# First layer, chunks 1 to 7: the next chunk's decoding asked for behind the first gate step instead of in front of it

## The chip, the cores and the metric

The kernel runs on one core of a Trainium2 chip. A core has five engines that work side by side, each through a queue of its own in the order in which its instructions stand there: PE (TensorE, matrix products), DVE (VectorE), ACT (ScalarE), POOL (GpSimd) and SP, which here only starts transfers. They meet through semaphores. The metric is the device time of one execution in microseconds (us); a smaller number is better.

## What is computed

Three things stand behind one another: attention over 4 batches of 8 heads (576 positions of 64 each) with a bias worked out from cumulative sums, then a gated feed-forward layer, then a second feed-forward layer. All of it is in single precision.

```
x = attention(q, k, v, s)                  # (4, 8, 576, 64)
x = x.transpose(0, 2, 1, 3)                # 2304 tokens x 512
g = x @ w_gate                             # first layer, 512 -> 1536
x = silu(g) * (x @ w_val) @ w_out          # 1536 -> 512
h = x @ w_in                               # second layer, 512 -> 2048
out = silu(h) @ w_out2                     # 2048 -> 512
```

## The kernel before, in words

PE reaches single precision with split operands: a number is held as a high and a low part, and a product takes three matmuls (lines 522, 523 and 524 in mm3). Weights are split into such parts in the kernel, and they arrive in a packed 64-bit form that must be decoded first.

The first layer goes batch by batch. Each batch has nine chunks of weights (L1): gv 0 to 2, o1 0, gv 3 and 4, o1 1, gv 5, o1 2. A gv chunk is four gate steps of 24 matmuls: twelve into a gate tile, twelve into a value tile (both named pgv, lines 522 to 524), 288 tokens wide. Behind a step come the activation (silu_mul: tanh on ACT, L532, then two products on DVE, L533 on the gate tile and L534 on the value tile) and the split of the result (ACT L112, POOL L536). An o1 chunk is eight down steps of 12 matmuls into tiles po, added up by ACT (L563) or DVE (L565). Chunks 0 to 8 belong to the first batch; in it the weights of each chunk are decoded and split, and stored to memory for the later batches, which only load them.

The attention of the next batch is worked on beside the first layer. At the start of a chunk PE computes one set of scores (psc, L218), which DVE scales, biases and reduces (L235, with a small second instruction per pass that reads the accumulator out); the exponentials are ACT's (L255). Score tiles have banks of their own. In chunks 2, 4 and 6 a set is taken in six DVE operations, in chunks 1, 3, 5 and 7 in ten.

The decoding of one chunk is asked for in w_ahead (w_split for the chunk after the running one, w_load for the one behind that). It has four pieces; a piece is two ACT instructions (L409, then L410 into a scratch tile dk) and two DVE instructions (L412 on dk, then L415, which ends the use of dk). Two cuts follow: a high part by ACT (L112, tile wt from wraw) and a low part by POOL (L501), and then two stores. For chunks 1 to 8 the scratch dk lies in PSUM, in a pool of four banks (ps_m) that gives pgv, po and dk their banks in turn, in the order in which the program asks for them:

```
        if 0 < c < len(L1):
            k = ps_m.tile([P, DW], F32, tag="m", name="dk").bitcast(U32)
        else:
            k = dec_p.tile([P, DW], U32, tag="dk", name="dk")
```

A tile may be written once whatever read the tile before it in that bank is done. PE's order is written out by hand in this part; ACT, DVE, POOL and SP are put in order by a scheduler, which takes its ranks from the order in which the program asks. The chunks' steps and the requests between them are listed in body, which the diff touches.

Of the kernel before, what the change touches and what calls it, by code (L numbers as in the profile page):

```python
# [66 lines left out]
def kernel(  # L67
# [305 lines left out]
    L1 = [("gv", 0), ("gv", 1), ("gv", 2), ("o1", 0), ("gv", 3), ("gv", 4), ("o1", 1), ("gv", 5), ("o1", 2)]  # L373
# [200 lines left out]
    def chunk_steps(c):  # L574
        kind, i = stream[c]
        if c == 0:
            return [lambda f=f, n=n: gate(c, f, f, *n) for f, n in ((1, both[0]), (0, both[1]), (1, both[1]))]
        if kind == "gv":
            return [lambda f=f, n=n: gate(c, 2 * i + f, f, *n) for f, n in order(2, both, "01"[i == NGV - 1])]
        return [lambda m=m, n=n: down(c, i, m, *n) for m, n in order(KD, both, "1")]  # L580
# [162 lines left out]
    def scores(u):  # L743
        x = units[u]
        fetch(u)
        if (*x, "e") not in st:
            masks(*x)
        score_mm(*x)
        for i in HALF[x[2]][0]:
            for f in (score_min, expo, inverse, first_keys, normal):  # L750
                f(*x, i)

    def transpose(u):
        turn_mm(*units[u])
        turned(*units[u], 0)
        turned(*units[u], 1)

    def value(u):
        value_mm(*units[u])
        x_high(*units[u])  # L760
        x_low(*units[u])
# [50 lines left out]
    def w_ahead(c):  # L812
        wst.pop(c - 1, None)
        if first[c + 1]:
            w_split(c + 1)
        else:
            w_load(c + 1)
        if first[c + 2]:
            w_load(c + 2)

    def body():
# [60 lines left out]
        for c in range(last):  # L882
            b = batch[c]
            cur = chunk_steps(c)
            at = {k: [] for k in range(5)}
            if b + 1 < B:
                k, u0 = c % len(L1), (b + 1) * H
                if k < H:
                    at[1 if c == 0 else 0].append(lambda x=u0 + k: scores(x))
                    if k > 1:  # L890
                        at[2].append(lambda x=u0 + k - 2: value(x))
                    if k > 0:
                        at[2].append(lambda x=u0 + k - 1: transpose(x))
                else:
                    at[1] += [lambda x=u0 + k - 2: value(x), lambda x=u0 + k - 1: transpose(x)]
                    at[3].append(lambda x=u0 + k - 1: value(x))
            for n, stp in enumerate(cur):
                if n == 0:
                    w_ahead(c)
                if n * 4 % len(cur) == 0:  # L900
                    todo = events.get(c * 4 + n * 4 // len(cur), [])
                    with tc.issue_after(w_last[0]) if todo else nullcontext():
                        with tc.issue_after(act_last[0]) if todo else nullcontext():
                            for f in todo:
                                f()
                if c == 0:
                    for p in at[n - 1] if n else []:
                        p()
                elif n * 4 % len(cur) == 0:
                    for p in at[n * 4 // len(cur)]:  # L910
                        p()
                stp()
            for p in at[4]:
                p()
# [107 lines left out]
        second_layer.close()  # L1022

    body()


# [42 lines left out]
```

## Time and profile before

| | us |
|---|---|
| time, median of 3 runs | 1009.34 |
| lowest and highest of the three | 1008.01, 1009.38 |
| the profiled execution, its own time | 1008.46 |
| span of that execution in the trace | 1006.1 |
| PE busy in the span | 989.1 (98%) |
| DVE, ACT, POOL busy | 560.2, 523.1, 592.1 |

The span starts with the first instruction in the trace and ends with the last; the execution's own time has 2.36 us around it. A time in a row is counted from the span's start. On the page, part 1 gives busy time, part 2 the same in 40 slices, part 4 the chain of work that ended last, and part 5 groups of instructions with the idle time before them and what ended it. The stretch that the change touches is the first batch's first layer, from 76 to about 202 us.

### The profile page before, as it was taken

The numbers are of one execution on the slowest core, as the hardware profiler recorded it, in microseconds if no ns is written. First come the engines' busy times: TensorE is split into PE (matmuls) and PEld (weight loads), VectorE is DVE, ScalarE is ACT, GpSimd is POOL, SyncE is SP. The second block draws the span as 40 slices with busy tenths as digits, with TensorE's granted clock in tenths as the row PEclk, the third lists the DMA queues.
The fourth block names the chain that finished last, engine by engine and source line by source line (L and its number), as shares of the span: only waits on it lengthen the run. The fifth ranks groups of instructions, "written<-read, shape, count | busy, mean of one in ns | idle before, by whom it ended". The sixth has DMA issues, their size and how long they took to land.

```text
span 1006.1 us, 19498 instructions
## 1 busy us (share of the span) xinstructions
PE 989.1 (98%) x6924; PEld 929.8 (92%) x6924; DVE 560.2 (56%) x1408; ACT 523.1 (52%) x1267; POOL 592.1 (59%) x748
## 2 busy tenths in 40 slices
PE   8998999999999999999999999999999999999998
PEld 6587889999898899899899999999999999999998
DVE  5878666635545544545542223366666667665555
ACT  5879887525766435665542543244534335543333
POOL 6966747515866655756551665356567458674445
PEclk9999999999999999999999999999999999999999
DMA  8898879667788799776768686797867866896662
GB/s 232 204 309 293 269 280 303 226 211 252 282 289 268 262 308 303 270 241 229 261 235 312 248 305 253 264 386 290 292 232 279 316 222 250 295 345 232 248 221 103
DMA packets 81617, 267.16 MB, mean 266 GB/s; under 512 B 9904, under 2 KB 29360, under 8 KB 66160
## 3 DMA queue, kind: packets, MB, share of 16 engines
q1 hardware_dynamic: 81376, 265.73, 75.6%
q8 instruction: 54, 0.88, 0.3%
q14 instruction: 43, 0.35, 0.1%
q10 hardware_dynamic: 144, 0.20, 0.1%
HBM read 208.15 MB, written 57.75 MB: 264 GB/s over the span
## 4 chain that ended last, share of the span: by engine, by line
PE 89%; ACT 4%; DVE 2%; issue 2%; DMA 2%; POOL 1%; POOLq 0%; DVEq 0%; ACTq 0%
PE pgv L522 9%; PE pgv L524 9%; PE pgv L523 9%; PE pu L664 6%; PE pu L668 6%; PE pu L667 6%; PE po L709 6%; PE po L710 6%; PE po L711 6%; PE po L522 5%; PE po L523 5%; PE po L524 5%; PE pv L351 4%; PE psc L218 4%; PE ptr L302 3%
## 5 line engine op out<-in xcount | busy, mean ns | idle before, releaser
L522 PE MATMUL pgv<-xt,wt 128*128 128x288 f32 x768 | 229.9, 299 | 4.6 <-DVE u L533 2.3
L524 PE MATMUL pgv<-xt,wt 128*128 128x288 f32 x768 | 226.2, 294 | 0.0
L523 PE MATMUL pgv<-xt,wt 128*128 128x288 f32 x768 | 226.1, 294 | 0.0
L522 PEld LDWEIGHTS pgv<-xt,wt 128*128 128x128 f32 x768 | 144.1, 188 | 16.4 <-DVE m L235 6.3
L641 POOL TENSOR_TENSOR h<-u,h 128x384 fp32r<-128x384 f32 x72 | 75.1, 1044 | 142.8 <-ACT h L112 134.9
L523 PEld LDWEIGHTS pgv<-xt,wt 128*128 128x128 f32 x768 | 144.1, 188 | 0.0
L524 PEld LDWEIGHTS pgv<-xt,wt 128*128 128x128 f32 x768 | 144.0, 188 | 0.0
L536 POOL TENSOR_TENSOR h<-u,h 128x288 fp32r<-128x288 f32 x96 | 79.1, 826 | 86.2 <-ACT h L112 84.6
L112 ACT ACTIVATE h<-u 128x288 fp32r<-128x288 f32 (+1 forms) x168 | 79.7, 475 | 96.3 <-DVE u L534 95.2
L522 PE MATMUL po<-h,wt 128*128 128x288 f32 x384 | 114.8, 299 | 0.0
L523 PE MATMUL po<-h,wt 128*128 128x288 f32 x384 | 113.1, 294 | 0.0
L524 PE MATMUL po<-h,wt 128*128 128x288 f32 x384 | 113.0, 294 | 0.0
L709 PE MATMUL po<-h,wt 128*128 128x384 f32 x336 | 112.4, 335 | 0.0
L664 PE MATMUL pu<-x,wt 128*128 128x384 f32 x330 | 111.8, 339 | 0.5 <-ACT s L670 0.5
L710 PE MATMUL po<-h,wt 128*128 128x384 f32 x336 | 112.3, 334 | 0.0
L711 PE MATMUL po<-h,wt 128*128 128x384 f32 x336 | 112.3, 334 | 0.0
L667 PE MATMUL pu<-x,wt 128*128 128x384 f32 x330 | 111.7, 339 | 0.0
L668 PE MATMUL pu<-x,wt 128*128 128x384 f32 x330 | 111.7, 339 | 0.0
L641 POOL TENSOR_TENSOR h<-t,h 128x384 fp32r<-128x384 f32 x96 | 106.6, 1131 | 5.5 <-ACT h L112 5.5
L255 ACT ACTIVATE e<-e,m 64x64 f32<-64x64 f32 (+4 forms) x160 | 88.3, 553 | 31.0 <-DVE m L235 30.2
L670 ACT ACTIVATE s<-pu 128x384 f32<-128x384 f32 x48 | 23.6, 492 | 150.5 <-PE pu L668 150.5
L720 DVE TENSOR_TENSOR acc<-po,acc 128x384 f32<-128x384 f32 x144 | 76.8, 558 | 36.3 <-PE po L711 35.6
(115 smaller groups left out, 2187.9 us busy)
## 6 DMA issues: line engine op xcount, KB each, us to landing
wt<-w_d SPq DMA_DIRECT2D x54, 1024.0 KB, 7.0
wt<-wu_d SPq DMA_DIRECT2D x48, 1024.0 KB, 9.3
wt<-wu_d SPq DMA_DIRECT2D x47, 768.0 KB, 6.5
r<-in_w_dram SPq DMA_DIRECT2D x36, 512.0 KB, 7.1
w_d<-wt SPq DMA_DIRECT2D x18, 1024.0 KB, 8.3
r<-in_w_dram SPq DMA_DIRECT2D x64, 256.0 KB, 7.3
qkr<-in_qk_dram SPq DMA_DIRECT2D x32, 288.0 KB, 8.2
cumb<-cum_d SPq DMA_DIRECT2D x15, 576.0 KB, 9.1
```

Source lines behind the costliest of these rows:

```text
L112: act_last[:] = [nc.scalar.activation(out=out, in_=in_, func=AF.Copy, scale=scale).ins]
L255: nc.scalar.activation(out=e[:r, hd, :wd], in_=e[:r, hd, :wd], func=AF.Exp, bias=m[hd][:r], scale=-1.0, accum_out=put[hd],)
L522: nc.tensor.matmul(out=ps[:, :n], lhsT=a, rhs=xh, start=(k == 0), stop=False)
L523: nc.tensor.matmul(out=ps[:, :n], lhsT=a, rhs=xl, start=False, stop=False)
L524: nc.tensor.matmul(out=ps[:, :n], lhsT=c, rhs=xh, start=False, stop=(k == last))
L641: nc.gpsimd.tensor_tensor(out=h[:, 1], in0=u, in1=h[:, 0].bitcast(F32), op=ALU.subtract)
L664: nc.tensor.matmul(out=o, lhsT=a, rhs=x[:, 0, kk], start=fresh and kk == 0, stop=False, skip_group_check=True)
L667: nc.tensor.matmul(out=o, lhsT=a, rhs=x[:, 1, kk], stop=False, **more)
L668: nc.tensor.matmul(out=o, lhsT=c, rhs=x[:, 0, kk], stop=kk == 1, **more)
L709: nc.tensor.matmul(out=ps, lhsT=a, rhs=h[:, 0], start=fresh, stop=False, skip_group_check=True)
L710: nc.tensor.matmul(out=ps, lhsT=a, rhs=h[:, 1], stop=False, **more)
L711: nc.tensor.matmul(out=ps, lhsT=c, rhs=h[:, 0], stop=e == 1, **more)
```

## The change

In each of the chunks 1 to 7 the request w_ahead(c) moves from in front of the chunk's first step to behind it. Since the next batch's score set is asked for with the first step, w_ahead(c) now also stands behind that set. Chunk 0 and all chunks from 8 on are as before. Nothing is added or taken away.

```
             for n, stp in enumerate(cur):
-                if n == 0:
+                if n == (1 if 0 < c < len(L1) - 1 else 0):
                     w_ahead(c)
                 if n * 4 % len(cur) == 0:
```

PE's instructions stand in the same order in both kernels. On DVE, ACT, POOL and SP the order differs between chunk 1 and chunk 8 and nowhere else. Since the banks are given out in the order of the requests, they differ too. Before, chunk 1 asks for four dk tiles and then for the two tiles of its first step, so the first step lies in banks that a dk has used, and so does the second. In the changed kernel the first step asks first, then the four dk tiles, then the second step: six requests over four banks, so that the second step gets the two banks of the first step, and what it waits for is L533 and L534 of that step. It is so in chunks 1, 2, 4, 5 and 7.

DVE in chunk 5, the part of its queue that ends with the first step's L533; e and m are the scores' results, wraw the decoded weights, r a packed piece. Before:

```order
L235 ISA m 128x1
L235 ISA e,m<-psc,e 128x64
L235 ISA m 128x1
L235 ISA e,m<-psc,e 128x64
L235 ISA m 128x1
L235 ISA e,m<-psc,cumb,m 128x448
L235 ISA m 128x1
L235 ISA e,m<-psc,e,m 128x64
L235 ISA m 128x1
L235 ISA e,m<-psc,cumb,m 128x448
L235 ISA m 128x1
L533 SCALAR_TENSOR_TENSOR u<-th,pgv 128x288
```

In the changed kernel, the rows that end with the same L533:

```order
L235 ISA m 128x1
L235 ISA e,m<-psc,e 128x64
L235 ISA m 128x1
L415 SCALAR_TENSOR_TENSOR wraw<-r_2198,dk 128x512
L235 ISA e,m<-psc,cumb,m 128x448
L235 ISA m 128x1
L412 SCALAR_TENSOR_TENSOR dk<-wraw,dk 128x512
L235 ISA e,m<-psc,e,m 128x64
L235 ISA m 128x1
L235 ISA e,m<-psc,cumb,m 128x448
L235 ISA m 128x1
L533 SCALAR_TENSOR_TENSOR u<-th,pgv 128x288
```

Before, the four decoded pieces of this chunk's turn stand wholly ahead of the rows shown; the last of their L415 comes right behind the set's first score pass. Now three L412 and two L415 stand among the set's first nine score passes, all ahead of L533, and one L412 and two L415 behind it.

DVE in chunk 2, at the score operations on 320 columns and the first step's L533. Before:

```order
L412 SCALAR_TENSOR_TENSOR dk<-wraw,dk 128x512
L235 ISA e,m<-psc,e 128x320
L235 ISA m 128x1
L235 ISA e,m<-psc,e 128x320
L235 ISA m 128x1
L415 SCALAR_TENSOR_TENSOR wraw<-r_1303,dk 128x512
L415 SCALAR_TENSOR_TENSOR wraw<-r_1305,dk 128x512
L533 SCALAR_TENSOR_TENSOR u<-th,pgv 128x288
```

In the changed kernel:

```order
L534 TENSOR_TENSOR u<-pgv,u 128x288
L412 SCALAR_TENSOR_TENSOR dk<-wraw,dk 128x512
L235 ISA e,m<-psc,e 128x320
L235 ISA m 128x1
L235 ISA e,m<-psc,e 128x320
L235 ISA m 128x1
L415 SCALAR_TENSOR_TENSOR wraw<-r_1397,dk 128x512
L412 SCALAR_TENSOR_TENSOR dk<-wraw,dk 128x512
L268 RECIPROCAL rl<-l 64x2
L268 RECIPROCAL rl<-l 128x2
L415 SCALAR_TENSOR_TENSOR wraw<-r_1399,dk 128x512
L533 SCALAR_TENSOR_TENSOR u<-th,pgv 128x288
```

Before, two L415 stand between the score operations and L533. Now two whole pieces do, L412 and L415 each, and the other two pieces follow behind L534.

## Rows read from the trace of the kernel before

**Rows 1.** The page, parts 1 and 4: busy time, chain
```profile
PE 989.1 (98%) x6924; PEld 929.8 (92%) x6924; DVE 560.2 (56%) x1408; ACT 523.1 (52%) x1267; POOL 592.1 (59%) x748
...
PE 89%; ACT 4%; DVE 2%; issue 2%; DMA 2%; POOL 1%; POOLq 0%; DVEq 0%; ACTq 0%
```

**Rows 2.** Stretches: length, busy time (instructions) per engine, granted clock, DMA
```profile
100.00:200.00 100.00, 100.00 (x778) 90.46 (x779) 64.94 (x190) 75.19 (x186) 62.70 (x93) 1.00 0.80 271
200.00:1006.00 806.00, 799.31 (x5455) 769.82 (x5453) 420.35 (x953) 371.12 (x884) 458.28 (x527) 1.00 0.74 265
```

**Rows 3.** PE's waits, 56 to 220 us: total, times, longest
```profile
PE pgv L522 <- DVE wraw L415: 2.3, 2, 1.9
PE pgv L522 <- DVE u L533: 0.7, 1, 0.7
```

**Rows 4.** Timeline of PEld (weight loads), starts of chunks 2, 4, 5
```profile
96.18 0.19 PEld L522 LDWEIGHTS pgv<-xt,wt 128*128 128x128 f32 x1 [2.39 <-DVE wraw L415]
...
100.00 0.19 PEld L522 LDWEIGHTS pgv<-xt,wt 128*128 128x128 f32 x1 [0.62 <-DVE wraw L415]
...
131.17 0.41 PEld L218 LDWEIGHTS psc<-qkr 64*128 64x128 f32 x6 [0.17 <-ACT acc L563]
...
132.45 0.19 PEld L522 LDWEIGHTS pgv<-xt,wt 128*128 128x128 f32 x1 [0.44 <-issue]
...
148.61 0.30 PEld L218 LDWEIGHTS psc<-qkr 64*128 64x128 f32 x4 [0.16 <-issue]
...
150.64 0.19 PEld L522 LDWEIGHTS pgv<-xt,wt 128*128 128x128 f32 x1 [0.76 <-DVE dk L412]
```

**Rows 5.** Timeline of PE: first matmuls of chunks 1 and 2
```profile
78.97 0.40 PE L522 MATMUL pgv<-xt,wt 128*128 128x288 f32 x1 [0.74 <-DVE u L533]
...
96.42 0.30 PE L523 MATMUL pgv<-xt,wt 128*128 128x288 f32 x1
...
97.47 0.30 PE L522 MATMUL pgv<-xt,wt 128*128 128x288 f32 x1
```

**Rows 6.** Timeline of DVE, chunk 5: score operations, then L533
```profile
151.02 0.50 DVE L235 CUSTOM_DVE_ANT_0 e<-psc,cumb 128x320 f32<-128x320 f32 x1
...
155.04 0.45 DVE L533 SCALAR_TENSOR_TENSOR u<-th,pgv 128x288 f32<-128x288 f32 x1
```

**Rows 7.** Timeline, second batch: score matmuls on PEld, first DVE operation
```profile
234.84 0.30 PEld L218 LDWEIGHTS psc<-qkr 64*128 64x128 f32 x4 [0.16 <-issue]
...
236.08 0.49 DVE L235 CUSTOM_DVE_ANT_0 e<-psc,cumb 128x320 f32<-128x320 f32 x1 [0.67 <-PE psc L218]
...
220.64 0.52 PEld L218 LDWEIGHTS psc<-qkr 64*128 64x128 f32 x8 [0.16 <-issue]
...
221.50 0.22 DVE L235 CUSTOM_DVE_ANT_0 e<-psc,e 64x64 f32<-64x64 f32 x1 [0.30 <-PE psc L218]
```

**Rows 8.** Timeline of DVE, chunk 2: score operations, then L533
```profile
99.27 1.27 DVE L415 SCALAR_TENSOR_TENSOR wraw<-r,dk 128x512 uint32<-128x512 uint32 x2
100.47 0.44 DVE L533 SCALAR_TENSOR_TENSOR u<-th,pgv 128x288 f32<-128x288 f32 x1
```

**Rows 9.** Groups of ACT by line and shape, 60 to 203 us: tanh
```profile
L532 ACT ACTIVATE th<-pgv 128x288 f32<-128x288 f32 x24 | 9.6, 402 | 6.3 <-PE pgv L524 6.3
```

**Rows 10.** Timeline of POOL: second cut for chunk 2
```profile
86.20 2.39 POOL L501 TENSOR_TENSOR wt<-wraw,wt 128x1024 fp32r<-128x1024 f32 x1 [0.67 <-POOL h L536]
```

**Rows 11.** Short stretches with granted clock, at start-up and chunk 2
```profile
14.00:18.00 4.00, 2.90 (x22) 2.15 (x24) 2.88 (x15) 3.42 (x9) 3.32 (x9) 0.79 0.98 334
18.00:22.00 4.00, 4.00 (x28) 2.37 (x26) 2.59 (x16) 2.71 (x12) 4.00 (x9) 0.78 1.05 222
...
94.00:98.00 4.00, 2.12 (x17) 1.82 (x14) 4.00 (x15) 3.57 (x7) 1.80 (x3) 1.00 0.85 326
```

More of the change, by code (lines that the diff above doesn't have):

```diff
@@ L897, in body @@
             for n, stp in enumerate(cur):
-                if n == 0:
+                if n == (1 if 0 < c < len(L1) - 1 else 0):
                     w_ahead(c)
```

## The prediction

> **What bounds the kernel now.** I read busy time and the chain first: PE works 989.1 of 1006.1 us, and 89% of the chain that ended last is PE's [rows 1]. So every microsecond by which PE is held up or let go in the first layer shows in the end, unless a later wait takes it up. The stretches leave little room for that: from 100 to 200 us PE is busy all the time, and from 200 to the end 799.31 of 806 us, all at a granted clock of 1.00 [rows 2]. PE's waits between 56 and 220 us are then the whole of what an edit here can win: 2.3 us in two waits for L415 and 0.7 us in one for L533 [rows 3]; a wait on the transposed scores of 0.6 us is not touched. These views count from the end of the modelled matmuls; the weight loads show the same waits a little longer, 2.39 us at 96.18 and 0.62 us at 100.00 [rows 4], and chunk 1 begins at 78.97 after 0.74 us [rows 5]. Of the 2.39, 0.44 is the plain gap behind a score set, since chunk 4 shows it with no wait at 132.45 [rows 4]. That leaves real stalls of 0.74, 1.95 and 0.62 us, together 3.3 us.
>
> **What the change takes away.** Asked for behind the first step, the decoding no longer stands in front of that step on ACT and DVE, and the first step no longer lies in banks that a dk has just used. So all three stalls go: -0.74 in chunk 1, -1.95 and -0.62 in chunk 2. Chunks 3 to 7 have no stall to lose.
>
> **What it adds.** The second step now gets the banks of the first. Its first matmul waits for L533 on the gate tile, its thirteenth for L534. That would cost nothing if DVE reached L533 at once: a step is 24 matmuls at 0.131 us, from eight of them between 96.42 and 97.47 [rows 5], so 3.2 us with the longer first one, and L533 has the second half of the step, 1.6 us, in which tanh and L533 (0.40 [rows 9] and 0.45 [rows 6]) fit. But DVE has a queue. Behind the score matmuls it must do the set's score operations and, among them, decoding operations, before L533. So the size of the new wait is the length of that queue.
>
> I take the prices from rows. In chunk 5 the first score operation starts at 151.02 and L533 at 155.04, DVE busy throughout, with nine score operations and, as the order shows, one L415 between [rows 6]; two L415 in a row take 1.20 us to the next start, 0.60 each [rows 8], so the nine score operations are 4.02 - 0.60 = 3.4 us. Some 0.3 of these are gaps in which DVE waits for its own small result; with other work between they fill up, so 3.1 to 3.4. A score set's first operation starts 1.24 us behind the set's first weight load in the ten-operation form (234.84 to 236.08) and 0.86 in the six-operation form (220.64 to 221.50), when DVE is free [rows 7]. PE goes from the set's first load to the step's first in 2.03 us (148.61 to 150.64) and 1.28 us (131.17 to 132.45) [rows 4].
>
> **Chunks 5 and 7.** Counted from the set's first load: DVE starts at 1.24, nine score and five decoding operations (5 x 0.60 = 3.0) take 6.1 to 6.4, L533 0.45, and 0.05 to the matmul (an estimate): 7.85 to 8.15. PE would have begun its second step at 2.03 + 3.2 = 5.24. The wait is 2.6 to 2.9, of which I take 2.6 in each, since rows of one engine overlap a little more the denser they stand.
>
> **Chunk 4** (six score operations with two L412 and two L415 among them. In chunk 2 the first four and an L412 take 98.45 - 97.01 = 1.44, so 0.84 without it, and the two on 320 columns 99.27 - 98.45 = 0.82 [rows 8]): 0.86 + 1.66 + 4 x 0.60 + 0.2 for two reciprocals + 0.5 = 5.6, against 1.28 + 3.2 = 4.5. Wait 1.1.
>
> **Chunk 1** starts 0.74 earlier, at 78.23. Here ACT comes late: the next batch's exponentials and scalings stand in front of its two L410, so the second ends at about 80.6 (an estimate, from the same instructions in chunk 1's trace), and then DVE has one L412, three short score operations (0.57), two L415 and one score operation on 448 columns (0.73 with its gap; both are parts of the 3.4 above) ahead of L533: 80.6 + 0.60 + 0.57 + 1.20 + 0.73 + 0.45 = 84.2, up to 84.7 if a piece slips. PE wants 78.23 + 3.2 = 81.46. I take 84.5, so +3.0. Its second half waits for L534, 1.95 behind L533 (two score passes and an L412 stand between), against half a step of 1.6: +0.3. Chunk 1 in all: -0.74 + 3.0 + 0.3 = +2.6.
>
> **Chunk 2**: it begins its score set 2.6 later, at 95.54, and its first step at 96.83 in place of 96.18. DVE begins at 96.4; four score operations (0.85), L534 (0.37), L412 and the two passes on 320 (1.42), L415, L412, a reciprocal, L415 (1.95), L533: 101.45, matmul at 101.5, against 96.83 + 3.2 = 100.04. So +1.5, and the lag behind the kernel before, which itself began this step at 100.00, is then 1.5: the chunk gives back 1.1.
>
> **Chunks 3 and 6** are down steps, whose next bank was a dk's. In chunk 3 the L415 that frees it is done some 0.4 us before PE comes: 0. In chunk 6 two such waits are about 0.6 together; between 0 and 1.2 by the same prices.
>
> **The sum.** 2.6 - 1.1 + 0 + 1.1 + 2.6 + 0.6 + 2.6 = +8.4 us. Behind chunk 8 PE is the bound and there is nothing to give the lag back. Against the profiled execution: 1008.46 + 8.4 = 1016.9; it lies 0.9 under the median of the runs, by which it would be 1017.7. I say 1017.2. The spread: if each of the five queues is 0.9 us shorter (a decoding operation and a half), 4.5 comes off, 1012.5; with the longer ends throughout (0.3 in chunks 5 and 7, 0.5 in chunk 1, 0.6 in chunk 6, half a microsecond in 2 and 4), 2.7 comes on, 1019.6.
>
> A rule of the Trainium skill bears on the new wait: "PSUM — Partial Sum Buffer", in its summary of rules for kernel authors, wants an engine that reads PSUM while matmuls run to have another bank than they write, and banks to be emptied promptly. The trace agrees as far as it goes: waits of PE there are for the last reader of the bank. By the rule alone the first step's early start would be bought by a late emptying, which has the sign of my sum and gives no size.
>
> **Rivals.**
> *Covered wait, faster.* If DVE came to L533 within the half step (its queue no longer than 1.6 us behind the first half), only the removal would be left: 1008.46 - 3.3 = 1005.2. For it: DVE is busy only 65 of 100 us from 100 to 200 [rows 2]. Against: it is busy throughout in just this stretch of chunk 5 [rows 6]. Chance 0.07.
> *Partly covered, no change.* If the stall came only in chunks 1 and 2, because later ones have DVE ahead of time, +1.5 is left: 1010.0. Chance 0.06.
> *Weights late, slower still.* The decoding, and with it the cuts, runs about a step later. In chunk 1 the second cut now ends at 88.59 (86.20 + 2.39 [rows 10]) for a chunk that begins at 96.18, with its second half needed 1.6 later. A step later it is some 92 to 95.4, and the changed kernel needs it at 98.4. It decides when POOL slips 3 us more behind its other work; then +1 to +3 in several chunks: 1018 to 1022. Chance 0.05.
> *Clock.* The granted clock was 0.79 and 0.78 in the two stretches behind 14 us, where PE was busy 2.90 of 4 us, and 1.00 from 94 to 98, where it was busy 2.12 of 4 with the longest wait so far [rows 11]. The fall cost 4 x 0.21 + 4 x 0.22 = 1.7 us of full speed. The new waits, 2.6 to 3.0, are longer than the 2.39 that did nothing. If one to four of them bring such a fall: 1018.9 to 1024. Chance 0.07. The Trainium skill, "TensorE: Matmul & The Clock Gate", Part 1, says that the throttled clock is the default and activity releases it; by it each new wait would be a candidate, the row at 94 says that a wait of that size need not be one.
> That the change does nothing is ruled out: DVE's queue does differ.
>
> **How the numbers follow.** Forecast 0.75, the rivals 0.07, 0.06, 0.05 and 0.07. A measurement of this kernel tells about 0.2%, 2 us, from no change. Slower by more: 0.75 + 0.05 + 0.07, less a little for a sum that is badly short, 0.86; within: 0.07; faster: 0.07. The range: 1011.5 to 1020.7, from a little under the short queues to one fall of the clock on top of the sum or the nearer half of late weights; what is left out is the covered cases and the far ends.
>
> **What would show it.** In the changed kernel PE should wait for L533 at the second step of chunks 1, 2, 4, 5 and 7 (3.0, 1.5, 1.1, 2.6, 2.6), the three waits of before should be gone, DVE should be busy without a gap ahead of each of those L533, and from 205 us on all rows should stand about 8.4 us later. I am wrong if PE does not wait there, if DVE idles ahead of L533 (then ACT or a bank holds it, not the queue), if PE waits for L501 (weights), or if the later batches give the lag back.

## The result: 1.25% slower, half as much again as the sum

| | before | changed |
|---|---|---|
| median, 6 runs each (us) | 1008.49 | 1020.42 |
| lowest and highest | 1006.23, 1009.38 | 1018.12, 1023.87 |
| ratio, 95% interval | | 1.0125 [1.0108, 1.0142] |
| profiled execution, span in its trace | 1008.46, 1006.1 | 1018.7, 1016.9 |
| mean granted clock of that trace | 0.998 | 0.991 |

The change costs 12.6 us (10.9 to 14.3 by the interval). The forecast was 8.4 us more than the kernel before, with a chance of 0.86 for slower. The sign and the mechanism came out, the size did not: 12.6 on the median of 1009.34 that the forecast stood on is 1022, beyond the range's upper end of 1020.7; the median measured beside 1008.49 is 1020.42, just under it. The difference is the granted clock.

The changed kernel's page, parts 1 and 4, to be held against [rows 1]: PE does the same 6924 matmuls in 995.6 us in place of 989.1, and the chain's share of PE rises from 89 to 90%.

```profile
PE 995.6 (98%) x6924; PEld 934.3 (92%) x6924; DVE 559.5 (55%) x1408; ACT 524.5 (52%) x1267; POOL 593.7 (58%) x748
...
PE 90%; DVE 4%; ACT 3%; issue 1%; POOL 1%; DMA 1%; POOLq 0%; DVEq 0%; ACTq 0%
```

What PE waited for between 56 and 230 us, to be held against [rows 3] (total, times, longest): L415 is gone from the list, and L533 stands there five times instead of once.

```profile
PE pgv L522 <- DVE u L533: 9.4, 5, 2.7
PE pv L351 <- ACT pt L112: 0.6, 1, 0.6
```

Where they are, by the weight loads of the changed kernel (start, length, engine, line, operation, and in brackets the idle time ahead and its releaser), to be held against [rows 4, 5]:

```profile
85.29 0.19 PEld L522 LDWEIGHTS pgv<-xt,wt 128*128 128x128 f32 x1 [2.88 <-DVE u L533]
...
87.13 0.29 PEld L522 LDWEIGHTS pgv<-xt,wt 128*128 128x128 f32 x1 [0.16 <-DVE u L534]
...
98.93 0.19 PEld L522 LDWEIGHTS pgv<-xt,wt 128*128 128x128 f32 x1 [0.44 <-DVE m L235]
...
103.56 0.19 PEld L522 LDWEIGHTS pgv<-xt,wt 128*128 128x128 f32 x1 [1.44 <-DVE u L533]
...
140.29 0.19 PEld L522 LDWEIGHTS pgv<-xt,wt 128*128 128x128 f32 x1 [1.06 <-DVE u L533]
...
161.08 0.19 PEld L522 LDWEIGHTS pgv<-xt,wt 128*128 128x128 f32 x1 [2.57 <-DVE u L533]
...
178.82 0.19 PEld L522 LDWEIGHTS po<-h,wt 128*128 128x128 f32 x1 [0.34 <-DVE wraw L415]
...
201.40 0.19 PEld L522 LDWEIGHTS pgv<-xt,wt 128*128 128x128 f32 x1 [2.58 <-DVE u L533]
```

These are the second steps of chunks 1, 2, 4, 5 and 7, the second half of chunk 1's, the first step of chunk 2, now at the plain 0.44, and a down step of chunk 6. Why they are as long as they are, DVE shows in chunk 5 (first score operation and L533):

```profile
154.52 0.49 DVE L235 CUSTOM_DVE_ANT_0 e<-psc,cumb 128x320 f32<-128x320 f32 x1 [0.67 <-PE psc L218]
...
160.58 0.45 DVE L533 SCALAR_TENSOR_TENSOR u<-th,pgv 128x288 f32<-128x288 f32 x1
```

Between them stand 6.06 us without a gap, nine score operations and five of the decoding, where [rows 6] had nine and one in 4.02.

DVE is not the only queue that is late. The tanh that this L533 needs runs on ACT here:

```profile
159.28 0.38 ACT L532 ACTIVATE th<-pgv 128x288 f32<-128x288 f32 x1
```

The first step begins at 155.31, and its first half is done about 1.6 us later, at 156.9 (an estimate from the length of a step). ACT comes to the tanh 2.4 us behind that, since three instructions of the decoding (two L409, one L410) stand ahead of it. It ends 0.91 before L533 starts; in chunks 1, 2, 4 and 7 that distance is 0.91, 0.71, 1.37 and 0.92. So DVE ends last, and DVE sets the wait. With DVE free at that moment ACT's queue alone would still have left waits of some 1.7 us in chunks 5 and 7 and 2.0 in chunk 1 (estimates, the waits less these distances).

And the stretches around three of the waits, with the granted clock as the third number from the end:

```profile
82.00:86.00 4.00, 1.35 (x10) 1.12 (x10) 4.00 (x16) 3.63 (x10) 0.59 (x3) 1.00 0.41 109
86.00:90.00 4.00, 4.00 (x21) 3.84 (x20) 3.60 (x11) 3.97 (x10) 3.94 (x5) 0.60 0.68 221
...
158.00:162.00 4.00, 1.66 (x12) 1.43 (x11) 4.00 (x15) 4.00 (x9) 0.10 (x1) 0.99 0.91 233
162.00:166.00 4.00, 4.00 (x21) 3.83 (x20) 2.00 (x6) 3.22 (x9) 4.00 (x6) 0.59 0.85 201
...
198.00:202.00 4.00, 1.65 (x13) 1.42 (x12) 4.00 (x17) 4.00 (x8) 0.00 (x0) 1.00 0.41 106
202.00:206.00 4.00, 4.00 (x22) 4.00 (x20) 2.37 (x8) 3.39 (x10) 3.80 (x5) 0.61 0.53 213
```

Behind the waits in chunks 1, 5 and 7 the granted clock is 0.60, 0.59 and 0.61 for a stretch of 4 us, that is the lower of its two levels, 1.2 GHz in place of 2.4, for most of it. With the neighbours (0.97 in the stretch behind 90 us, 0.99 from 158, 0.97 behind 206) that is 1.72, 1.68 and 1.68 us of full speed, 5.1 together. Behind the shorter waits of chunks 2 and 4 it stays at 1.00.

So the trace's account is: waits that came 2.88 + 0.16 + 1.44 + 1.06 + 2.57 + 0.34 + 0.17 (a second one in chunk 6, for L565) + 2.58 = 11.2; waits that went 3.3; clock 5.1; a chunk 1 whose score set starts 1.05 late out of the start-up (77.18 in place of 76.13), which the change does not touch: together 14.0. At start-up this execution had the low clock for longer than the one of the kernel before, 0.64 and 0.51 in the two stretches where [rows 11] has 0.79 and 0.78:

```profile
14.00:18.00 4.00, 3.46 (x24) 2.50 (x26) 2.36 (x11) 2.86 (x7) 1.57 (x5) 0.64 0.96 319
18.00:22.00 4.00, 4.00 (x21) 1.83 (x18) 2.14 (x14) 1.79 (x8) 4.00 (x9) 0.51 1.05 222
```

That is 3.4 us of full speed in place of 1.7, and part of the distance between the two mean clocks in the table. The lag in the rows is 13.5, half a microsecond less than that sum: one and the same L533 of the second batch stands at 225.57 in the kernel before and at 239.09 in the changed one. Later 2.7 us come back, most of it at a wait for L533 of 1.55 us at 404.41 in the kernel before that the changed kernel's trace does not have. 10.8 us are left between the two spans.

One correction of the part on the kernel: the four banks are not handed out strictly in turn. By a strict turn the third dk of chunk 5 would lie in the bank of the first step's gate tile. But ACT's L410 writes that dk at 158.15, before L533 reads the gate tile at 160.58. So the four dk of a chunk take two banks by turns, and the second step takes those that the first step's tiles had. The prediction used this as the programs have it.

### The profile page after: what moved, and what is told of

Its sections match the earlier page's. It is cut to its first block, busy times and chain, and to the rows that moved or that the text cites. A ratio compares the mean times of both kernels' runs of the same rounds, so it can differ in the third digit from the quotient of the medians.

```text
span 1016.9 us, 19485 instructions
## 1 busy us (share of the span) xinstructions
PE 995.6 (98%) x6924; PEld 934.3 (92%) x6924; DVE 559.5 (55%) x1408; ACT 524.5 (52%) x1267; POOL 593.7 (58%) x748
## 4 chain that ended last, share of the span: by engine, by line
PE 90%; DVE 4%; ACT 3%; issue 1%; POOL 1%; DMA 1%; POOLq 0%; DVEq 0%; ACTq 0%
PE pgv L522 9%; PE pgv L524 9%; PE pgv L523 9%; PE pu L664 6%; PE pu L668 6%; PE pu L667 6%; PE po L709 6%; PE po L710 6%; PE po L711 6%; PE po L522 5%; PE po L523 5%; PE po L524 5%; PE pv L351 5%; PE psc L218 4%; PE ptr L302 3%; DVE e L235 1%
## 5 line engine op out<-in xcount | busy, mean ns | idle before, releaser
L522 PEld LDWEIGHTS pgv<-xt,wt 128*128 128x128 f32 x768 | 145.8, 190 | 21.8 <-DVE u L533 10.7
L523 PEld LDWEIGHTS pgv<-xt,wt 128*128 128x128 f32 x768 | 146.0, 190 | 0.0
L524 PEld LDWEIGHTS pgv<-xt,wt 128*128 128x128 f32 x768 | 146.0, 190 | 0.0
L536 POOL TENSOR_TENSOR h<-u,h 128x288 fp32r<-128x288 f32 x96 | 79.2, 826 | 86.2 <-ACT h L112 81.6
L116 POOL TENSOR_SCALAR e<-e,rl 128x128 f32<-128x128 f32 (+8 forms) x135 | 72.7, 552 | 46.6 <-DVE rl L268 45.4
```

The source lines that it names most:

```text
L522: nc.tensor.matmul(out=ps[:, :n], lhsT=a, rhs=xh, start=(k == 0), stop=False)
L523: nc.tensor.matmul(out=ps[:, :n], lhsT=a, rhs=xl, start=False, stop=False)
L524: nc.tensor.matmul(out=ps[:, :n], lhsT=c, rhs=xh, start=False, stop=(k == last))
```

## The experiments

Theory: the bank that the second step gets is the first step's, emptied by an L533 that stands at the end of DVE's queue, and a long wait brings the clock down behind it. Rival "load": decoding among the scores holds PE by the work itself, whichever bank is used. Rival on the clock: its falls have another cause or cost nothing. In the times below "over" is the ratio to the kernel before in runs on the same chip, times its median.

### The value half done twice: does the wait bring the clock down?

```diff
+            if c in (1, 5, 7) and t == 1 and f_in == 0 and n0 == 0:
+                mm3(ps, wst[c], xs, n0, n)
```

> The changed kernel, with the twelve matmuls of the value half of the first step done twice in chunks 1, 5 and 7: 36 matmuls more, 1.6 us in each of the three, on PE's path just ahead of its long wait. The second pass starts its tile anew. Theory of the clock (the wait of 2.3 us and more without a matmul brings the granted clock down behind it): the three waits shrink to about 1 us, the second step begins when it did, the clock behind stays at 1.00, and the time falls by some 5 us, to 7 to 9 over the kernel before, although PE does more. Rival (the low clock behind these places has another cause, or costs nothing): 12 to 13 over the kernel before or more.

Measured: 1015.16 us, 1.0078 [1.0060, 1.0096] of the kernel before, 7.9 us over, against 12.6 for the changed kernel. 36 matmuls more made it 4.7 us faster. Weight loads at the second step of chunk 5, and the stretches that showed 0.59 and 0.61:

```profile
153.56 0.19 PEld L522 LDWEIGHTS pgv<-xt,wt 128*128 128x128 f32 x1 [0.76 <-DVE m L235]
...
159.33 0.19 PEld L522 LDWEIGHTS pgv<-xt,wt 128*128 128x128 f32 x1 [0.99 <-DVE u L533]
...
162.00:166.00 4.00, 4.00 (x41) 3.23 (x41) 1.41 (x4) 2.41 (x6) 4.00 (x9) 1.00 0.73 240
...
202.00:206.00 4.00, 4.00 (x42) 3.54 (x39) 0.98 (x3) 1.74 (x4) 4.00 (x8) 1.00 0.93 329
```

The second step begins 5.77 us behind the first, to the hundredth as in the changed kernel (155.31 to 161.08). Nothing was won in the chunk itself. PE is merely idle for 0.99 instead of 2.57 us ahead of it, and the clock stays at 1.00. The gain agrees with the price of the three falls, 5.1, less a longer wait for L534 in chunk 1 (1.02 in place of 0.16). It is not this one execution: the six runs with the matmuls done twice have mean clocks of 0.996 to 0.998, the six of the changed kernel 0.988 to 0.993. The clock is a cost of its own, and it hangs on the wait.

The control, the same edit on the kernel before:

> The kernel before with the value half of the first step done twice in chunks 1, 5 and 7, 36 matmuls more, as in the run on the changed kernel. PE has no wait there that could take them up: 3 x 1.6 = 4.8 us over the kernel before by every theory of a kernel bound by PE. It is the control for the same edit on the changed kernel.

Measured: 1009.83 us, 1.0022 [1.0012, 1.0032], 2.2 us over and not 4.8. "By every theory" was too bold: PE does have waits there. With twelve matmuls more in chunk 1 the wait of 1.88 us at chunk 2's start shrinks to 0.37, the one of 0.39 behind it is gone, and the one at 404 shrinks from 1.55 to 0.18; in chunk 1 itself a wait of 0.74 grows to 1.50, and one of 0.61 is new. On its own the edit makes a kernel slower, so what it won on the changed kernel came from the wait that it filled.

### The second step in banks of its own: bank or load?

```diff
+        two = None
+        if c in (1, 2, 4, 5, 7) and (f_in, n0) == ((1, 0) if c == 7 else (0, HB)):
+            two = ps_a.tile([P, 2, 512], F32, tag="a", name="pgv")
...
-            ps = ps_m.tile([P, 512], F32, tag="m", name="pgv")
+            ps = ps_m.tile([P, 512], F32, tag="m", name="pgv") if two is None else two[:, t]
```

> The changed kernel, with the two tiles of the second step in chunks 1, 2, 4, 5 and 7 placed in the score sets' own PSUM pool instead of the four shared banks. The late request and what DVE has to do stay. The second step then waits for the passes over the set's first tile, which stand 2 to 3 us ahead of L533 in DVE's queue. Theory of the banks (it is the bank of the first step's gate tile, emptied only behind DVE's queue, that holds PE): the five waits for L533 go, at most 0.4 us is left in chunk 1, no fall of the clock in this stretch; the waits of the kernel before stay away too, so 1 to 3 us under the kernel before, less what the turn of the banks brings at the value or transpose tiles (up to 1 us each). Rival, load (late decoding holds PE by DVE's work itself): the waits move and their sum stays, 8 us and more over the kernel before.

> The same, in chunks 5 and 7 alone. Chunks 1, 2 and 4 keep their waits for L533 (3.0, 1.4 and 1.1 us in the changed kernel's trace) and chunk 1 its fall of the clock (1.7 us); chunks 5 and 7 lose 2.6 us and 1.7 us each. So by queue, banks and clock the changed kernel less 8.6, some 4 us over the kernel before. By the rival, load, 8 us and more over the kernel before, as the kernel with all five.

Measured: in all five chunks 1014.62 us, 1.0063 [1.0042, 1.0083], 6.4 us over; in chunks 5 and 7 alone 1014.28 us, 1.0065 [1.0042, 1.0087], 6.6 over. In the second kernel, what PE waited for from 56 to 230 us, and DVE's first score operation and L533 in chunk 5:

```profile
PE pgv L522 <- DVE u L533: 4.7, 3, 2.7
PE po L522 <- DVE acc L568: 1.9, 1, 1.9
...
```

```profile
154.02 0.49 DVE L235 CUSTOM_DVE_ANT_0 e<-psc,cumb 128x320 f32<-128x320 f32 x1 [0.67 <-PE psc L218]
...
160.09 0.45 DVE L533 SCALAR_TENSOR_TENSOR u<-th,pgv 128x288 f32<-128x288 f32 x1
```

DVE's queue is the same to the hundredth (6.07 us from the first row to the second, 6.06 in the changed kernel), L533 ends at 160.54, and PE had begun the step at about 158.0 (3.2 behind the first step at 154.82) with no wait. The two waits of chunks 5 and 7 are gone, and the clock stays at 1.00 from 90 us on. The bank makes this wait; DVE's load alone does not. The second kernel is 6.0 us faster than the changed one, where the rows give 6.2: 4.7 of waits and 3.4 for two falls gone, 1.9 of a new wait come. The times are 8 and 2.5 us above what I expected, the first nearly as high as the rival had it, and that has a place: the banks turn differently behind the edit, and a down step of chunk 6 now waits 1.9 us for the adder of a tile before it (L565; the edit moves it to L568); with five chunks changed the transposes wait as well (1.37, 1.20 and 0.90 us behind scores and L534) and one fall of the clock, 0.60 behind 90 us, follows two such waits. With five chunks changed no wait for L533 is left, but the waits at other places come to some 7.5 us where the changed kernel had 9.4. So which tile waits is shown to be the bank's doing. By the time alone the rival is not beaten: most of the waiting found another place, as it had said.

### The scratch tile out of the four banks

```diff
-        if 0 < c < len(L1):
+        if c < 0:
```

> The changed kernel, with the decoding's scratch tile dk of chunks 1 to 8 in SBUF, as chunk 0 has it, instead of in the four PSUM banks. Theory of the banks (the second step waits for L533 because the four dk hand it the banks of the first step): the five waits for L533 in chunks 1, 2, 4, 5 and 7 are gone, with them the falls of the granted clock, and so are the three waits of the kernel before (3.3 us): 2 to 4 us under the kernel before. Rival, load (decoding work on DVE and ACT behind the score set holds PE whichever bank is used): waits of 2 us and more stay in chunks 1, 5 and 7, 8 to 14 us over the kernel before.

> The kernel before, with dk in SBUF in the same way. Theory of the banks: its waits for L415 at 96.18 and 100.00 and for L533 at 78.97 are waits for a bank, so all three go: 2 to 4 us under the kernel before, and the same as the late kernel with dk in SBUF, since the place of the request then matters to PE no more. Rival, load: the same as the kernel before within 1 us.

Measured: late 1020.22 us, 1.0129 [1.0106, 1.0152]; early 1018.17, 1.0095 [1.0075, 1.0114]. My times fell flat, both of them. The waits at the places named are gone, in both, but others came. The late one's waits, and its two decoding lines on DVE (busy time, mean ns):

```profile
PE pv L351 <- DVE u L533: 5.7, 3, 2.5
PE ptr L302 <- DVE m L235: 1.5, 1, 1.5
PE pgv L522 <- ACT acc L563: 1.2, 1, 1.2
PE ptr L316 <- ACT dk L410: 1.1, 1, 1.1
...
```

```profile
L415 DVE SCALAR_TENSOR_TENSOR wraw<-r,dk 128x512 uint32<-128x512 uint32 x28 | 23.6, 856 | 0.2
L412 DVE SCALAR_TENSOR_TENSOR dk<-wraw,dk 128x512 uint32<-128x512 uint32 x28 | 20.8, 761 | 8.2 <-ACT wraw L409 5.4 <-ACT dk L410 2.6
```

The decoding costs DVE more with dk in SBUF (L415 856 ns, it was 683; L412 761, it was 690), 7 us in all over the chunks from 76 to 203 us. And without the four dk in the round the value tile (L351) comes upon a bank that an L533 has not left. So this pair tells neither theory from the other by its time: it swapped one turn of the banks for another. The edit was too coarse, and the next run made it in one chunk only:

```diff
-        if 0 < c < len(L1):
+        if 0 < c < len(L1) and c != 3:
```

> The kernel before, with dk in SBUF for the four pieces decoded in chunk 2 alone (those of chunk 3's weights). Theory of the banks: the waits for L415 at 96.18 and 100.00 go, 2.6 us; the four pieces cost DVE 4 x 0.25 = 1.0 us more, from the rows of the kernels with dk in SBUF; 1 to 2.6 us under the kernel before, if the turn of the banks behind them makes no new wait. Rival, load: the two waits stay.

Measured: 1008.55 us, 1.0013 [1.0002, 1.0023], 1.3 over. The waits for L415 are gone here too. PE waits for L533 and L534 instead, 0.16, 1.03, 0.36, 0.94 and 0.18 us between 79 and 105, together 2.7 where it had been 3.0. In this kernel a bank taken off one tile is missed by the next.

### The request in single chunks, and one step later

The changed kernel's condition cut to chunk 5, and to chunk 2:

```diff
-                if n == (1 if 0 < c < len(L1) - 1 else 0):
+                if n == (1 if c == 5 else 0):
```

> The change in chunk 5 alone. Theory of queue and clock: one wait for L533 of about 2.6 us at the second step of chunk 5 and a stretch at about 0.6 of the clock behind it, so 2.6 + 1.6 = 4.2 us over the kernel before, 2 less if a later wait gives it back. Without a cost of the clock 2.6. Rival, load: with the other chunks as before DVE comes into chunk 5 with nothing behind, so under 1 us.

Measured: 1012.59 us, 1.0045 [1.0029, 1.0062], 4.5 over. One wait of 2.35 us at 157.79 and a clock of 0.63 behind it: the price that the whole change has in this chunk, wait and clock, alone. (In that trace a wait of 1.87 us at chunk 2's start, as the kernel before has it, brought a fall as well.)

The same line with c == 2:

> The change in chunk 2 alone. Theory of queue and clock: the waits of 1.95 and 0.62 us at its first and second step go, a wait for L533 of about 1.4 us comes at its second step (the whole change shows 1.44 there with 1.00 of the clock behind it), so 1.1 us under the kernel before, up to 2.5 under it where the wait of 1.9 us in the kernel before has brought the clock down. Rival, load: the later decoding makes the chunks behind late, 1 us and more over the kernel before.

Measured: 1010.47 us, 1.0036 [1.0022, 1.0049], 3.6 over. Wrong by 4.7. PE's row at chunk 2's second step, DVE's L533 of the chunk before, and the stretches around:

```profile
100.89 0.61 PE L522 MATMUL pgv<-xt,wt 128*128 128x288 f32 x1 [3.09 <-DVE u L533]
```

```profile
95.21 0.45 DVE L533 SCALAR_TENSOR_TENSOR u<-th,pgv 128x288 f32<-128x288 f32 x1 [2.16 <-POOL h L536]
```

```profile
98.00:102.00 4.00, 1.11 (x4) 1.11 (x5) 3.83 (x12) 4.00 (x17) 0.72 (x2) 0.78 0.18 52
102.00:106.00 4.00, 4.00 (x18) 4.00 (x18) 2.42 (x6) 4.00 (x11) 3.20 (x5) 0.50 0.73 222
```

The wait is 3.09, not 1.4, and the clock 0.50 behind it; this execution is the slowest of the six. In the whole change chunk 2 comes 2.75 us later, and that L533, at 97.12, is ahead of the score set, which starts at 97.64; here L533 of the chunk before waits 2.16 us for POOL's L536, and the score passes stand behind it on DVE. So the price of a late request is not one number for a chunk. It depends on what the chunk before has left in the queues.

```diff
-                if n == (1 if 0 < c < len(L1) - 1 else 0):
+                if n == (2 if 0 < c < len(L1) - 1 else 0):
```

> The request for the next chunk's decoding behind the second step of chunks 1 to 7, in place of behind the first. Theory of the banks: the second step then does not come on the first step's banks, and the third comes on those of a dk, so the long waits for L533 at the second step are gone and waits for L415 at the third and fourth step of a microsecond or less take their place; no fall of the clock; within 3 us of the kernel before, unless the weights come late (a wait for L501 or the high part by L112 at the next chunk's start). Rival, load (decoding among or behind the score operations holds PE in any case): waits of 2 us and more in chunks 1, 5 and 7 and falls of the clock behind them, 8 us and more over the kernel before.

Measured: 1014.23 us, 1.0072 [1.0060, 1.0084], 7.3 over, between both. No wait for L533 at any second step. PE waits for L415, at the third step of chunk 1 for 2.33 us (with the clock at 0.65 behind it) and at the attention's value tiles (L351) of chunks 4, 5 and 7 for 1.15 to 1.23; in chunk 2 such a tile waits 1.55 us for L534. The bank theory named the third step of chunk 1, and my size for it was too small: I had let it wait a microsecond at most. The value tiles I had not named.

### Is POOL behind the wait of the kernel before?

```diff
-            engines[WL[phase[c]][e]].tensor_tensor(out=wl, in0=t, in1=wh.bitcast(F32), op=ALU.subtract)
+            (nc.vector if (c, e) == (2, 1) else engines[WL[phase[c]][e]]).tensor_tensor(out=wl, in0=t, in1=wh.bitcast(F32), op=ALU.subtract)
```

> The kernel before, with one cut of the weights for chunk 2, the second (POOL from 86.20 for 2.39 us), on DVE instead of POOL. Theory: the kernel before waits at 96.18 because POOL is behind: its L536 at 91.08 frees u, L533 on DVE waits 2.4 us for that, L410 on ACT waits for the bank that this L533 empties, and L415 and PE wait in turn. With 2.4 us taken off POOL the wait of 1.9 us at 96.18 is gone or under 0.5 us: 1.5 to 2.5 us under the kernel before. Rival (the decoding itself is late whatever POOL does): the same as the kernel before or slower by the 1 to 2 us that DVE takes for the cut.

Measured: 1006.86 us, 0.9997 [0.9986, 1.0008]: no difference that can be told, where I had expected 1.5 to 2.5 us less. PE's two waits in chunk 2:

```profile
95.39 0.40 PE L522 MATMUL pgv<-xt,wt 128*128 128x288 f32 x1 [0.89 <-DVE wraw L415]
...
99.61 0.40 PE L522 MATMUL pgv<-xt,wt 128*128 128x288 f32 x1 [0.79 <-DVE wraw L415]
```

The wait of 1.88 is 0.89 now, and that of 0.39 has become 0.79. POOL had a share in the first, and 0.40 of the 0.99 won is lost again a step later.

> The change in chunk 2 alone, with the same cut on DVE. With the change in chunk 2 alone the wait for L533 was 3.1 us and not 1.4. Theory: POOL again, since that L533 and the score passes stood behind an L533 of the chunk before that waited 2.2 us for L536. With the cut off POOL the wait at the second step of chunk 2 is that of chunk 4, 0.8 to 1.2 us, with no fall of the clock behind it, and the time lies 1 us under to 1 us over the kernel before. Rival: the wait stays near 3 us and the time 3 us over.

Measured: 1008.59 us, 1.0018 [1.0006, 1.0029], 1.8 over. The wait is 2.32, down from 3.09 but not to 1.2, since the L533 ahead of it still waits 2.12 us for L536. The clock stays at 1.00 in the profiled execution. Less POOL work helps in the direction foreseen. How far the wait is POOL's is not settled.

No kernel that was run beats the kernel before by more than can be told.

## Why the prediction was right and wrong

- **What bounds it.** Right. Every wait of the first layer arrives in the end but for 2.7 us, the part that I had said had nothing to give it back. One wait of 1.55 us at 404 did, since the rows of PE's waits that I read ended at 220 us; [rows 2] had shown the 6.7 us of idle time behind 200, and I passed over them.
- **What goes.** Right: 0.74, 1.95 and 0.62 us are gone.
- **What comes.** Right in place and number, and nearly so in size. Chunk 1: 3.0 and 0.3 said, 2.88 and 0.16 measured. Chunk 2: 1.5, 1.44. Chunk 4: 1.1, 1.06. Chunk 5: 2.6, 2.57. Chunk 6: 0.6 in two waits for a dk said, 0.34 for L415 and 0.17 for L565 measured. Chunk 7: 2.6, 2.58. The sum of 8.4 stands against 7.9. DVE's prices from [rows 6, 8] were enough for it: 6.1 to 6.4 us said for the fourteen operations of chunk 5, 6.06 measured. The runs with banks of their own show that it is the bank. One premise was wrong without harm to the sum: the prediction had the tanh done at once within the half step, and in chunk 5 it came 2.4 us later on ACT. It did not show, because DVE was later still by 0.91. Two small slips in the working change nothing: 78.23 + 3.2 is 81.43 and not 81.46, and 1016.9 less 4.5 is 1012.4 and not 1012.5.
- **The clock. This is the step that failed.** I gave it no term in the sum and a chance of 0.07 as a rival, on the row from 94 to 98 us, where 2.39 us of waiting had left the clock at 1.00 [rows 11]. Three of five new waits brought a fall, 5.1 us by the rows and 4.7 by the run with the value half twice. The price was right, 1.7 each, from the start-up's rows. What was wrong was to take one wait without a fall as the rule. The falls had to be in the sum for the three long waits, at 5 us: 8.4 + 5 = 13.4 where 12.6 was measured. That these two lie so near is in part luck: without the 2.7 us that came back the sum would be 10.7, beside 10.2 between the two profiled executions. The kernel before is not free of falls either: in its runs beside the experiments the mean clock goes from 0.994 to 0.998, and the one trace that was read, with 0.998, stands at the upper end.
- **What the Trainium skill says of it** ("TensorE: Matmul & The Clock Gate", Part 1), that the throttled clock is the default and activity releases it, was the better guide here: each long wait was a candidate, as the sentence in the prediction had it. The trace agrees with it by the three stretches at about 0.6.
- **The other rivals.** The covered wait did not come: from a set's first score operation to L533, DVE had no gap but one of 0.24 us in chunk 1, behind ACT's L410. The partly covered one did not come: chunks 4, 5 and 7 have their waits. Late weights did not either: POOL's second cut for chunk 2 ends at 93.91 + 2.40 = 96.31, and the chunk began at 98.93. I had said up to 95.4 and 98.4 for when they are needed.

## What to carry to other kernels

A request that is moved in program order moves its scratch tiles in their pool as well. Before such a move, write down which tile hands its bank to whom and what stands ahead of that reader in its engine's queue: the wait is that queue's length less the time that PE is still busy. Summed from rows it came within 0.15 us here; in the run with the change in chunk 2 alone it did not, since the chunk before had left other work in the queues. Look at every engine that the reader needs, here ACT's tanh too. Then ask of each long wait on TensorE what the clock does behind it, and put the fall into the sum and not among the accidents; where such a wait cannot be avoided, more matmuls put into it can pay even if their results are of no use: 36 of them made the changed kernel 4.7 us faster.

## What the runs showed of the hardware

- The falls of TensorE's clock do not follow from the length of the wait alone. From 56 us on, in the profiled executions, counted by the matmuls (which show a wait some 0.2 us shorter than the weight loads do), PE's waits of 2.65, 2.71, 3.09 and 3.17 us were each followed by one; of 1.87, 2.33, 2.34, 2.35 (in two places) and 2.47 too; of 1.88, 1.89, 1.90, 2.32 and 2.48 not. Of single waits up to 1.78 none was, but two of 1.37 and 1.18 close together were; two of 1.49 and 1.11, as close, in the kernel with the late request and dk in SBUF, were not. What else decides is open.
- Part of the spread of the runs is open as well. The changed kernel's six runs go from 1018.12 to 1023.87 with mean clocks from 0.988 to 0.993, and two of the same 0.993 differ by 2.5 us. The clock at start-up is one source: in nine of the fourteen profiled executions its fall between 14 and 26 us cost 1.7 us of full speed, in five 3.4.
- With dk in SBUF, L412 and L415 take two SBUF inputs. Then L415 took 856 ns in place of 683, L412 761 in place of 690, and POOL's L536 beside them 912 in place of 804. The Trainium skill, "SBUF — State Buffer", section "Who interferes with whom", says that a DVE instruction with two SBUF inputs contends with GpSimd instructions that read SBUF. The three rows agree with that; no run here took the two engines apart.
